# Block-causal attention and a feed-forward layer: splits, last blocks and a weight cast on other engines

## The chip, the cores and the metric

The kernel runs on one core of a Trainium2 chip, in one launch. Its engines work side by side, each through its own queue in order: TensorE (PE; its weight loads are listed as PEld), VectorE (DVE), ScalarE (ACT), GpSimd (POOL), and SyncE (SP), which here issues the DMAs. The metric is the device time of one execution in microseconds (us); less is better.

## The reference

Eight batches of eight heads, 576 tokens, 64 columns a head. The mask lets a block of 64 tokens see itself and all blocks before it. The attention's output, heads side by side (4608 x 512), goes through a layer of 2048 columns with a piecewise activation.

```python
scores = (1 / sqrt(64)) * q @ k.T              # per head, 576 x 576
scores = where(block_i >= block_j, scores, -1e9)   # blocks of 64
attn = exp(scores - max); attn /= (sum + 1e-9)
x = (attn @ v)  -> transposed to 4608 x 512
h = x @ w_in                                   # 512 x 2048
g = where(h >= 1, h, where(h <= -1, 0, (h + 1)**2 / 4))
out = g @ w_out                                # 2048 x 512
```

All inputs and the output are float32.

## The kernel before

Matrix products run on a shorter float type (fp32r). To keep precision, most operands are split into an upper part (hi, a cast) and a lower part (lo, the value minus its upper part), and a product is summed from hi and lo products. A split is thus always two operations, a cast and a subtraction, on the engines named in the code.

**Attention.** `Pair` is one batch and two heads; there are 32 pairs, worked through in eight steps each by `attention_steps`. For a pair, q and k are loaded as [128, 9, 64] (eight tiles for the two heads and a ninth for the two last blocks of 64 tokens), split by `split_q` and `split_k` on DVE (k's lower part on POOL, for the first pair on DVE), and transposed on PE by `turned` (two heads, q and k) and `turned_last` (the ninth tile). Each result lands in a PSUM bank and is copied by ACT into `qb` or `kb`; the half that holds one part is copied once more into `qa` or `ka`, by a DMA for `turned` and by DVE (L371) for `turned_last`. `qa` and `ka` also carry four rows with the mask. `product` sums two matmuls into the scores. `scores(j, g)` takes a head j and a group g of query tiles (g 0 holds 128 and 256 columns, g 1 holds 384, g 2 holds 512), `scores_last` the two heads' last blocks: a maximum by DVE (L414, L438, L442), the exponential by ACT (L418, L444), sum, EPS, reciprocal and scaling by DVE (L400, L401, L424, L448, L450). The probabilities `pr` are moved by a DMA into fp32r tiles (not for the first batch, which transposes `pr` itself), transposed by `turn` and `turn_last` (`ps_t`), and split for the product with v (`ps_av`, L500). Inside `turn_last` the last 64 columns go into a bank of their own and from there to `pc`. The first two batches (`plain`) keep the probabilities in one float32 part.

**Weights.** `convert` turns a 64-bit weight piece of 128x256 into hi and lo: a DMA, two ACT scalings (L165, L166), three DVE operations (L167, L170, L173), an addition on POOL (L179), the upper part's cast on ACT (L181), and the lower part's subtraction on POOL (L183). There are 64 pieces; they run beside the first pairs, 24 in the first 36 steps and the other 40 in the following 24 steps. Pieces have rings of three buffers. w_in stays in SBUF (`wih`, `wil`), w_out's parts go back to DRAM and are read again for each step.

**Feed-forward.** From step 36 on each attention step is followed by one step of the feed-forward: `ffn_in` (twelve matmuls into `ph`, activation by ACT and DVE, a split by ACT and POOL, L646 to L661) and, for the step before, `ffn_out` (twelve matmuls into `po`, L670 and L675). What is left runs after the attention.

**Order.** A scheduler places the instructions of each engine from their priorities in program order and from when buffers come free. Each engine then runs its list strictly in that order and waits where an operand isn't there. PSUM banks come from `work_bank`: while the feed-forward hasn't started, banks alternate between a ring of four (`po`) and a ring of three (`work`); later all come from the ring of three. `pr` has three buffers.

Of the kernel before, what the change touches and what calls it, by code (L numbers as in the profile page):

```python
# [8 lines left out]
F32 = mybir.dt.float32  # L9
# [14 lines left out]
def block_attn_then_ffn(  # L24
# [9 lines left out]
    nc = tc.nc  # L34
# [117 lines left out]
    def convert(n, source, hi, lo, done):  # L152
# [28 lines left out]
        nc.scalar.copy(hi(), w32)  # L181
# [69 lines left out]
    class Pair:  # L251
# [52 lines left out]

        def split_q(self):

            qn = self.nat.pop("q")[:, : 2 * NTL + 1, :]
            self.qs = att1.tile([P, 2 * NTL + 1, 2, D], F32R, tag="qs", name="qs")
            for c0, c1 in ((0, 2 * NTL), (2 * NTL, 2 * NTL + 1)):
                nc.vector.tensor_scalar_mul(self.qs[:, c0:c1, 0, :], qn[:, c0:c1, :], SCALE)  # L310
            nc.vector.scalar_tensor_tensor(
                out=self.qs[:, :, 1, :], in0=qn, scalar=SCALE,
                in1=self.qs[:, :, 0, :].bitcast(F32), op0=ALU.mult, op1=ALU.subtract,
            )

        def split_k(self):
            kn = self.nat.pop("k")[:, : 2 * NTL + 1, :]
            self.ks = att1.tile([P, 2 * NTL + 1, 2, D], F32R, tag="ks", name="ks")
            for c0, c1 in ((0, 2 * NTL), (2 * NTL, 2 * NTL + 1)):
                nc.vector.tensor_copy(self.ks[:, c0:c1, 1, :], kn[:, c0:c1, :])  # L320
            (nc.vector if self.first else nc.gpsimd).tensor_tensor(
                out=self.ks[:, :, 0, :], in0=kn, in1=self.ks[:, :, 1, :].bitcast(F32),
                op=ALU.subtract,
            )
# [16 lines left out]
        def turned(self, is_q, j):  # L341

            src, a, bt, hi0 = (self.qs, qa, qb, 0) if is_q else (self.ks, ka, kb, D)
            ps = work_bank("ps_qk")
            for t in range(NTL):
                nc.tensor.transpose(  # L346
                    ps[:, t * P : (t + 1) * P].bitcast(F32R), src[:, j * NTL + t, :, :], ident_r
                )

            turned = ps[:, :SM].rearrange("p (t c) -> p c t", t=NTL)  # L350
            nc.scalar.copy(bt[:, j, :SM].rearrange("p (c t) -> p c t", t=NTL), turned)  # L351
            if self.first and j == 0:
                nc.vector.tensor_copy(
                    a[:D, j, :SM].rearrange("p (c t) -> p c t", t=NTL), turned[hi0 : hi0 + D]
                )
            else:
                nc.sync.dma_start(
                    a[:D, j, :SM].bitcast(F32), bt[hi0 : hi0 + D, j, :SM].bitcast(F32)
                )

        def turned_last(self):
# [6 lines left out]
            for i, (a, bt, hi0) in enumerate(((qa, qb, 0), (ka, kb, D))):  # L368
                blocks = ps[:, i * P : (i + 1) * P].rearrange("p (h c) -> p h c", h=2)
                nc.scalar.copy(last_blocks(bt), blocks)  # L370
                nc.vector.tensor_copy(last_blocks(a)[:D], blocks[hi0 : hi0 + D])  # L371
# [55 lines left out]
        def scores_last(self):  # L427
# [14 lines left out]
            nc.vector.tensor_tensor(out=nm[:, 2:3], in0=nm[:, 0:1], in1=nm[:, 1:2], op=ALU.min)  # L442
# [5 lines left out]
            nc.vector.tensor_tensor(out=sm[:, 2:3], in0=sm[:, 0:1], in1=sm[:, 1:2], op=ALU.add)  # L448
            self.inverse(sm[:, 2:3])
# [15 lines left out]
        def turn(self, j, g):  # L465
# [4 lines left out]
            for c0 in range(0, n, P):  # L470
                self.transposed(ps[:, c0 : c0 + P], pr, c0, P)
            if g == 0:
# [8 lines left out]
        def turn_last(self):  # L481
            pr = self.pr.pop("last")
            ps = work_bank("ps_t")
            for c0 in range(0, SM, P):
# [4 lines left out]
            )  # L489
# [82 lines left out]
    def attention_steps():  # L572
# [11 lines left out]
        for i, cur in enumerate(pairs + [None]):  # L584
# [42 lines left out]
            cur.scores(1, 2)  # L627
            cur.attn_v(0)
            cur.turn(1, 0)
# [131 lines left out]
```

## Time and profile before

| | before |
|---|---|
| median of 3 runs | 1270.86 us (1270.6 to 1273.3) |
| the profiled execution | 1272.09 us |
| its span in the profile | 1270.3 us |
| granted PE clock, mean | 0.985 |
| busy in the span | PE 95%, PEld 80%, DVE 67%, ACT 55%, POOL 36% |

The profile is of one execution. A row of the groups gives the source line, the engine, the operation with output and input, the count, busy time in us, the mean ns of one, and behind the second bar how long the engine stood idle just before and what released it. A row of the waits gives the engine and line that waited, the one that released it, the total us, how often, and the longest. A row of the windows gives for a stretch of the span the busy us of PE, PEld, DVE, ACT and POOL with instruction counts, the granted PE clock, the share of the DMA engines and GB/s. A row of the timeline begins with the start and the duration in us. "idle" of an engine that nobody waits for costs nothing.

### The profile page before, as it was taken

The page shows a single profiled execution, that of the slowest core. Times are in us where ns is not written, and L with a number is a line of the kernel's source. Part 1 is how long each engine was busy: PE and PEld are TensorE (multiplying, and loading weights), DVE is VectorE, ACT ScalarE, POOL GpSimd, SP SyncE. Part 2 cuts the span into 40 slices and gives each one's busy share as a digit, 9 for nine tenths or more (in the row PEclk, how much of TensorE's full clock was granted, in tenths as well). Part 3 has the DMA queues.
Part 4 walks back from the last instruction along what each step waited for, and adds up shares of the span by engine and source line. Part 5 has one row for each costly group of instructions (what it writes and reads, how often), then busy time and mean ns, then how long its engine had stood idle before and what let it go on. Part 6 is the DMA issues. An engine that isn't in the chain of part 4 may idle for free.

```text
span 1270.3 us, 20591 instructions
## 1 busy us (share of the span) xinstructions
PE 1210.7 (95%) x6496; PEld 1018.4 (80%) x6496; DVE 856.4 (67%) x2164; ACT 701.3 (55%) x1827; POOL 456.3 (36%) x454
## 2 busy tenths in 40 slices
PE   5879887899999999999999999999999999999998
PEld 4667666688888888888888888888888888888886
DVE  8998877857776777777777777777777676222222
ACT  5877656546565655566556656555565564222222
POOL 3555655523332333333333333333333332222222
PEclk9888989899999999999999999999999999999999
DMA  5656666655444545564455545454445443322432
GB/s 157 182 165 213 196 228 210 212 184 173 148 152 147 191 144 161 158 193 149 148 162 168 178 141 161 153 181 143 152 154 184 151 132 117 127 92 97 133 100 100
DMA packets 146093, 201.30 MB, mean 158 GB/s; under 512 B 63152, under 2 KB 93872, under 8 KB 145984
## 3 DMA queue, kind: packets, MB, share of 16 engines
q1 hardware_dynamic: 145984, 199.98, 50.4%
q8 instruction: 52, 0.85, 0.3%
q14 instruction: 57, 0.47, 0.1%
HBM read 120.59 MB, written 17.83 MB: 109 GB/s over the span
## 4 chain that ended last, share of the span: by engine, by line
PE 68%; DVE 8%; ACT 4%; issue 3%; DMA 3%; POOL 2%; SPq 0%; ACTq 0%; POOLq 0%; DVEq 0%
PE ph L646 26%; PE po L670 16%; PE po L675 8%; PE ps_av L500 7%; PE ps_t L461 3%; PE ps_s L394 3%; PE ps_s L391 3%; ACT pr L418 2%; PE ps_qk L346 2%; DMA prr<-pr 2%; DVE t L656 2%; DVE nm L414 1%; DVE t L659 1%; DVE pr L424 1%; POOL work L179 1%
## 5 line engine op out<-in xcount | busy, mean ns | idle before, releaser
L661 POOL TENSOR_TENSOR gl<-t,gh 128x512 fp32r<-128x512 f32 x144 | 186.9, 1298 | 604.7 <-ACT gh L660 301.8
L670 PE MATMUL po<-wo,gh 128*128 128x512 f32 x1152 | 296.9, 399 | 0.1
L656 DVE SCALAR_TENSOR_TENSOR t<-t 128x512 f32<-128x512 f32 x144 | 112.9, 784 | 200.2 <-ACT t L655 198.5
L646 PE MATMUL ph<-xh,wih 128*128 128x512 f32 x576 | 237.6, 413 | 2.7 <-DVE t L659 1.8
L670 PEld LDWEIGHTS po<-wo,gh 128*128 128x128 f32 x1152 | 207.7, 188 | 39.3 <-ACT gh L660 0.6
L646 PE MATMUL ph<-xl,wih 128*128 128x512 f32 x576 | 227.4, 395 | 0.9 <-DVE xl L536 0.9
L646 PE MATMUL ph<-xh,wil 128*128 128x512 f32 x576 | 227.4, 395 | 0.0
L655 ACT ACTIVATE t<-ph 128x512 f32<-128x512 f32 x144 | 86.1, 598 | 184.7 <-PE ph L646 184.7
L418 ACT ACTIVATE pr<-ps_s,nm 128x128 f32<-128x128 f32 (+3 forms) x256 | 134.4, 529 | 50.6 <-DVE nm L414 50.3
L414 DVE TENSOR_REDUCE nm<-ps_s 128x1 f32<-128x128 f32 (+3 forms) x256 | 123.6, 485 | 48.7 <-PE ps_s L394 47.4
L675 PE MATMUL po<-wo,gl 128*128 128x512 f32 x576 | 155.3, 391 | 0.0
L660 ACT CAST gh<-t 128x512 fp32r<-128x512 f32 x144 | 89.6, 622 | 102.1 <-DVE t L659 101.7
L391 PE MATMUL ps_s<-ka,qa 68*128 68x288 f32 (+4 forms) x384 | 122.5, 334 | 9.1 <-ACT kb L351 4.2
L646 PEld LDWEIGHTS ph<-xh,wil 128*128 128x128 f32 x576 | 109.1, 189 | 24.1
L675 PEld LDWEIGHTS po<-wo,gl 128*128 128x128 f32 x576 | 108.1, 188 | 23.3
L646 PEld LDWEIGHTS ph<-xh,wih 128*128 128x128 f32 x576 | 109.1, 189 | 21.7 <-DVE t L659 2.4
L646 PEld LDWEIGHTS ph<-xl,wih 128*128 128x128 f32 x576 | 109.6, 190 | 20.2 <-DVE xl L536 1.5
L394 PE MATMUL ps_s<-kb,qb 128*128 128x288 f32 (+4 forms) x384 | 121.4, 323 | 0.0
L454 ACT CAST pb<-ps_t 128x512 fp32r<-128x512 f32 (+1 forms) x120 | 65.5, 546 | 85.6 <-PE ps_t L461 83.8
L424 DVE TENSOR_SCALAR pr<-pr,sm 128x128 f32<-128x128 f32 (+3 forms) x256 | 104.8, 430 | 4.0
L336 POOL TENSOR_TENSOR vsr<-vn,vsr 64x64 fp32r<-64x64 f32 (+1 forms) x96 | 72.8, 768 | 88.6 <-ACT vsr L335 88.6
L456 DVE TENSOR_TENSOR pb<-ps_t,pb 128x512 fp32r<-128x512 f32 (+1 forms) x120 | 75.6, 630 | 40.4 <-ACT pb L454 39.9
(101 smaller groups left out, 1961.4 us busy)
## 6 DMA issues: line engine op xcount, KB each, us to landing
wo<-wo_split SPq DMA_DIRECT2D x144, 512.0 KB, 3.4
prr<-pr SPq DMA_DIRECT2D x96, 192.0 KB, 2.7
prr<-pr SPq DMA_DIRECT2D x72, 256.0 KB, 2.6
out_dram<-ob SPq DMA_DIRECT2D x36, 256.0 KB, 3.9
qn<-in_q_dram SPq DMA_DIRECT2D x32, 256.0 KB, 2.9
kn<-in_k_dram SPq DMA_DIRECT2D x32, 256.0 KB, 2.9
bits<-in_moe_w_in_dram SPq DMA_DIRECT2D x32, 256.0 KB, 3.6
bits<-in_moe_w_out_dram SPq DMA_DIRECT2D x32, 256.0 KB, 3.2
```

Of the source, the lines that this page charges most:

```text
L391: nc.tensor.matmul(ps, qa[:KA, j, c0 : c0 + P], ka[:KA, j, k0 : k0 + n], start=first, stop=False)
L394: nc.tensor.matmul(ps, qb[:, j, c0 : c0 + P], kb[:, j, k0 : k0 + n], start=False, stop=last)
L414: nc.vector.tensor_reduce(out=nm[:, i : i + 1], in_=ps[:, cs], axis=AX.X, op=ALU.max, negate=True)
L418: nc.scalar.activation(pr[:, cs], ps[:, cs], AF.Exp, bias=nm[:, i : i + 1], scale=1.0, accum_out=sm[:, i : i + 1],)
L424: nc.vector.tensor_scalar_mul(pr[:, cs], pr[:, cs], sm[:, i : i + 1])
L500: nc.tensor.matmul(ps[:, lo_col:], vt, x, start=first and i == 0 and m == 0, stop=last and i == len(parts) - 1 and m == len(mov) - 1,)
L646: nc.tensor.matmul(ph, w[:, cc, fs], x[:, cc, xs], start=(cc == 0 and i == 0), stop=(cc == NCC - 1 and i == 2),)
L656: nc.vector.scalar_tensor_tensor(out=t_, in0=t_, scalar=1.0, in1=t_, op0=ALU.min, op1=ALU.mult)
L660: nc.scalar.copy(gh, t_)
L661: nc.gpsimd.tensor_tensor(out=gl, in0=t_, in1=gh.bitcast(F32), op=ALU.subtract)
L670: nc.tensor.matmul(po[tt], gh[:, ts_], wo[:, w, :], start=(fc == 0 and w == 0), stop=False)
L675: nc.tensor.matmul(po[tt], gl[:, ts_], wo[:, 0, :], start=False, stop=fc == NFC - 1)
```

## The change

- The split of q no longer scales: `split_qk` casts the raw value on DVE in one instruction of [128, 9, 64] (before: 8 tiles and the ninth apart), and the lower part of q is subtracted on POOL, as k's already was; the first pair keeps both on DVE. The factor 1/8 is applied by ACT when it evicts the transposed q.
- `turned_last`: the second copy of the last blocks is made by a DMA instead of by DVE (the first pair keeps DVE).
- `scores_last`: the minimum of two columns and the sum with EPS become forms with a column as a scalar; sum and EPS are one instruction.
- The transposes of the last 64 columns move from `turn_last` into `turn(1, 0)`, into free columns of its bank; `attn_v(0)` is called after `turn(1, 0)`.
- In `convert` the cast of the upper part goes from ACT to POOL.

```diff
@@ convert
-        nc.scalar.copy(hi(), w32)
+        nc.gpsimd.tensor_copy(hi(), w32)
@@ class Pair
+        def split_qk(self, name, side):
+            x = self.nat.pop(name)[:, : 2 * NTL + 1, :]
+            parts = att1.tile([P, 2 * NTL + 1, 2, D], F32R, tag=name + "s", name=name + "s")
+            hi, lo = parts[:, :, side, :], parts[:, :, 1 - side, :]
+            nc.vector.tensor_copy(hi, x)
+            (nc.vector if self.first else nc.gpsimd).tensor_tensor(
+                out=lo, in0=x, in1=hi.bitcast(F32), op=ALU.subtract
+            )
+            return parts
+
         def split_q(self):
-            qn = self.nat.pop("q")[:, : 2 * NTL + 1, :]
-            self.qs = att1.tile([P, 2 * NTL + 1, 2, D], F32R, tag="qs", name="qs")
-            for c0, c1 in ((0, 2 * NTL), (2 * NTL, 2 * NTL + 1)):
-                nc.vector.tensor_scalar_mul(self.qs[:, c0:c1, 0, :], qn[:, c0:c1, :], SCALE)
-            nc.vector.scalar_tensor_tensor(
-                out=self.qs[:, :, 1, :], in0=qn, scalar=SCALE,
-                in1=self.qs[:, :, 0, :].bitcast(F32), op0=ALU.mult, op1=ALU.subtract,
-            )
+            self.qs = self.split_qk("q", 0)
@@ turned
-            nc.scalar.copy(bt[:, j, :SM].rearrange("p (c t) -> p c t", t=NTL), turned)
+            scale = SCALE if is_q else 1.0
+            nc.scalar.mul(bt[:, j, :SM].rearrange("p (c t) -> p c t", t=NTL), turned, scale)
@@ turned_last
-                nc.scalar.copy(last_blocks(bt), blocks)
-                nc.vector.tensor_copy(last_blocks(a)[:D], blocks[hi0 : hi0 + D])
+                nc.scalar.mul(last_blocks(bt), blocks, 1.0 if i else SCALE)
+                if self.first:
...
+                else:
+                    nc.sync.dma_start(
+                        last_blocks(a)[:D].bitcast(F32), last_blocks(bt)[hi0 : hi0 + D].bitcast(F32)
+                    )
@@ scores_last
-            nc.vector.tensor_tensor(out=nm[:, 2:3], in0=nm[:, 0:1], in1=nm[:, 1:2], op=ALU.min)
+            nc.vector.tensor_scalar(
+                out=nm[:, 2:3], in0=nm[:, 0:1], scalar1=nm[:, 1:2], scalar2=None, op0=ALU.min
+            )
...
-            nc.vector.tensor_tensor(out=sm[:, 2:3], in0=sm[:, 0:1], in1=sm[:, 1:2], op=ALU.add)
-            self.inverse(sm[:, 2:3])
+            nc.vector.tensor_scalar(
+                out=sm[:, 2:3], in0=sm[:, 0:1], scalar1=sm[:, 1:2], scalar2=EPS,
+                op0=ALU.add, op1=ALU.add,
+            )
+            nc.vector.reciprocal(sm[:, 2:3], sm[:, 2:3])
@@ turn
+            if j == 1 and g == 0:
+                ps_c = ps[:BLK, n : n + P]
+                self.transposed(ps_c, self.pr.pop("last"), SM, BLK)
+                self.split(
+                    ps_c.rearrange("p (h c) -> p h c", h=2), *(x[:BLK] for x in self.pc)
+                )
@@ turn_last
-            ps = work_bank("ps_t")
-            self.transposed(ps[:BLK, :P], pr, SM, BLK)
-            self.split(
-                ps[:BLK, :P].rearrange("p (h c) -> p h c", h=2), *(x[:BLK] for x in self.pc)
-            )
@@ attention_steps
             cur.scores(1, 2)
+            cur.turn(1, 0)
             cur.attn_v(0)
-            cur.turn(1, 0)
```

The scheduler places everything anew, so the lists of the engines differ throughout. Three places follow. The new lines have other numbers: L310 and L311 are the cast and subtraction of `split_qk`, L342 is L346, L395 and L398 are L391 and L394, L422 is L418, L450 is L444, L463 is L454, L472 is L463, L348 is L351.

POOL, in the third pair, while weights are converted; of before:

```order
L321 TENSOR_TENSOR ks<-kn,ks 128x9x64
L179 TENSOR_TENSOR work<-work,bits 128x256 x2
L183 TENSOR_TENSOR ws<-work,ws 128x256
L179 TENSOR_TENSOR work<-work,bits 128x256 x2
L183 TENSOR_TENSOR ws<-work,ws 128x256
L183 TENSOR_TENSOR wil<-work,wih 128x256
```

and of the change:

```order
L179 TENSOR_TENSOR work<-work,bits 128x256
L181 CAST ws<-work 128x256
L311 TENSOR_TENSOR qs<-qn,qs 128x9x64
L183 TENSOR_TENSOR ws<-work,ws 128x256
L179 TENSOR_TENSOR work<-work,bits 128x256
L181 CAST ws<-work 128x256
L183 TENSOR_TENSOR ws<-work,ws 128x256
L311 TENSOR_TENSOR ks<-kn,ks 128x9x64
```

The cast L181 stands between addition and subtraction of its piece, and the subtraction of q has come into the list ahead of that of k.

ACT, in the second pair, from the eviction of its first transposed probabilities (`pa`) on; of before:

```order
L454 COPY pa_527<-ps_t 128x384
L418 ACTIVATE pr,sm<-ps_s,nm 128x512
L165 ACTIVATE work<-bits 128x256
L454 COPY pb_529<-ps_t 128x3x128
L181 CAST wih<-work 128x256
L166 ACTIVATE bits<-bits 128x256
L351 CAST qb<-ps_qk 128x512
L444 ACTIVATE pr,sm<-ps_s,nm 128x288 x2
L454 COPY pb_529<-ps_t 128x4x128
L181 CAST wih<-work 128x256
L418 ACTIVATE pr,sm<-ps_s,nm 128x128
```

and of the change:

```order
L463 COPY pa_521<-ps_t 128x384
L422 ACTIVATE pr,sm<-ps_s,nm 128x512
L463 COPY pb_523<-ps_t 128x3x128
L450 ACTIVATE pr,sm<-ps_s,nm 128x288 x2
L348 ACTIVATE qb<-ps_qk 128x512
L422 ACTIVATE pr,sm<-ps_s,nm 128x128
L422 ACTIVATE pr,sm<-ps_s,nm 128x256
L463 COPY pb_523<-ps_t 128x4x128
```

The two casts L181 are gone, the scalings L165 and L166 stand elsewhere, and the exponentials of `scores_last` (128x288) come ahead of q's eviction.

PE, in the second pair, from the scores of 384 columns of its second head on (`ps_t` of 64x128 are the transposes of the last 64 columns, `ps_qk` from `ks` those of the next pair's k); of before:

```order
L394 MATMUL ps_s<-kb,qb 128x384
L646 MATMUL ph<-xh,wil 128x512
L463 MATMUL ps_t<-ident_r,pr 128x128 x4
L463 MATMUL ps_t<-ident_r,pr 64x128
L346 MATMUL ps_qk<-ident_r,ks 128x128 x4
L391 MATMUL ps_s<-ka,qa 128x512
L394 MATMUL ps_s<-kb,qb 128x512
L463 MATMUL ps_t<-ident_r,pr 128x128 x3
```

and of the change:

```order
L398 MATMUL ps_s<-kb,qb 128x384
L342 MATMUL ps_qk<-ident_r,ks 128x128 x4
L472 MATMUL ps_t<-ident_r,pr 128x128 x4
L395 MATMUL ps_s<-ka,qa 128x512
L398 MATMUL ps_s<-kb,qb 128x512
L472 MATMUL ps_t<-ident_r,pr 128x128 x3
L472 MATMUL ps_t<-ident_r,pr 64x128
```

K's transposes now stand ahead of those of the last blocks' probabilities (`turn_last`), and the last 64 columns come behind the transposes of `turn(1, 0)`. The later pairs have the same order here, with matmuls of the feed-forward between: of before, k's transposes in the middle of an `ffn_in`; of the change, a whole `ffn_in` between k's transposes and the scores of 512 columns.

More of the change, by code (lines that the diff above doesn't have):

```diff
@@ L303, in load @@
             self.nat[name] = t_
-        def split_q(self):
-            qn = self.nat.pop("q")[:, : 2 * NTL + 1, :]
-            self.qs = att1.tile([P, 2 * NTL + 1, 2, D], F32R, tag="qs", name="qs")
-            for c0, c1 in ((0, 2 * NTL), (2 * NTL, 2 * NTL + 1)):
-                nc.vector.tensor_scalar_mul(self.qs[:, c0:c1, 0, :], qn[:, c0:c1, :], SCALE)
-            nc.vector.scalar_tensor_tensor(
-                out=self.qs[:, :, 1, :], in0=qn, scalar=SCALE,
-                in1=self.qs[:, :, 0, :].bitcast(F32), op0=ALU.mult, op1=ALU.subtract,
-            )
-        def split_k(self):
[L317 to L323, printed above, removed]
-            )
+        def split_qk(self, name, side):
[7 more added lines that the diff above has]
+            return parts
+        def split_q(self):
+            self.qs = self.split_qk("q", 0)
+        def split_k(self):
+            self.ks = self.split_qk("k", 1)
         def split_v(self):
@@ L471, in turn @@
                 self.transposed(ps[:, c0 : c0 + P], pr, c0, P)
+            if j == 1 and g == 0:
[3 more added lines that the diff above has]
+                    ps_c.rearrange("p (h c) -> p h c", h=2), *(x[:BLK] for x in self.pc)
+                )
             if g == 0:
@@ L481, in turn_last @@
         def turn_last(self):
-            pr = self.pr.pop("last")
+            pr = self.pr["last"]
             ps = work_bank("ps_t")
```

7 lines of the change are left out of this document (4 added, 3 removed).

## The prediction, made before the changed kernel was run

> **What bounds the kernel now.** I read the page first (its first line is quoted), then the busy time of each engine by stretch (the next lines, from the windows).
>
> ```profile
> span 1270.3 us, 20591 instructions
> core 0: us, PE busy (x) PEld busy (x) DVE busy (x) ACT busy (x) POOL busy (x), PEclk, DMA share, GB/s
> 0.00:128.00 128.00, 99.19 (x514) 80.35 (x515) 112.78 (x341) 93.76 (x280) 63.42 (x85) 0.91 0.60 178
> 128.00:256.00 128.00, 109.92 (x528) 85.81 (x528) 101.42 (x247) 79.12 (x224) 75.03 (x90) 0.95 0.68 216
> 256.00:640.00 384.00, 380.88 (x2164) 325.74 (x2162) 271.42 (x694) 224.53 (x579) 126.13 (x115) 1.00 0.52 162
> ```
>
> The reader is to see two stages. From 256 us on TensorE (PE) is busy 99% of the time: 384 - 380.88 leaves 3.1 us in that stretch. The change removes no matmul, so little can be won there. In the first 256 us, while the weights are converted beside attention, PE stands idle (128 - 99.19) + (128 - 109.92) = 28.8 + 18.1 = **46.9 us**, and its granted clock is 0.91 and 0.95. DVE is busy 112.78 + 101.42 = 214 us of them, 84%. A gain has to come from those 46.9 us. Next, what PE waited for there (25 rows; the first, some of the next, and the last):
>
> ```profile
> PE ps_qk L346 <- DVE ident_r L89: 7.6, 1, 7.6
> PE ps_t L463 <- DVE sm L400: 7.4, 3, 3.8
> PE ps_s L391 <- ACT kb L351: 4.2, 2, 3.9
> ...
> PE ps_qk L346 <- ACT pc L454: 0.2, 1, 0.2
> ```
>
> Summed over all 25 rows, 25.3 us end on DVE (7.6 of them are the start), 19.9 on ACT and 1.1 on a DMA. No one transfer or engine is late: both engines serve long queues in order, and PE gets its operand when its turn comes.
>
> **DVE's own work.** Groups of DVE instructions in the first 256 us:
>
> ```profile
> L167 DVE TENSOR_SCALAR work<-work 128x256 f32<-128x256 f32 x64 | 29.5, 465 | 12.6 <-ACT work L165 11.8 <-POOL wil L183 0.7
> L311 DVE SCALAR_TENSOR_TENSOR qs<-qn,qs 128x576 fp32r<-128x576 f32 x9 | 7.5, 830 | 0.0
> L310 DVE TENSOR_SCALAR qs<-qn 128x512 fp32r<-128x512 f32 x9 | 4.2, 468 | 0.2 <-DMA qn<-in_q_dram 0.2
> L320 DVE CAST ks<-kn 128x512 fp32r<-128x512 f32 x9 | 4.0, 439 | 0.0
> L320 DVE CAST ks<-kn 128x64 fp32r<-128x64 f32 x9 | 2.7, 301 | 2.1 <-DMA kn<-in_k_dram 2.1
> L310 DVE TENSOR_SCALAR qs<-qn 128x64 fp32r<-128x64 f32 x9 | 2.5, 277 | 0.0
> L371 DVE CAST ka<-ps_qk 64x128 fp32r<-64x128 f32 x8 | 2.3, 293 | 0.6 <-ACT kb L370 0.4
> L371 DVE CAST qa<-ps_qk 64x128 fp32r<-64x128 f32 x8 | 2.2, 272 | 0.0
> L442 DVE TENSOR_TENSOR nm<-nm 128x1 f32<-128x1 f32 x8 | 2.1, 268 | 0.0
> L448 DVE TENSOR_TENSOR sm<-sm 128x1 f32<-128x1 f32 x8 | 2.1, 261 | 3.0 <-ACT pr L444 3.0
> L400 DVE TENSOR_SCALAR sm<-sm 128x1 f32<-128x1 f32 x39 | 5.6, 144 | 2.4 <-ACT pr L418 2.1
> ```
>
> The q and k splits cost 7.5 + 4.2 + 4.0 + 2.7 + 2.5 = 20.9 us for nine pairs. Eight of these pairs keep two casts of 128x576 on DVE. Scaled from the 128x512 cast, one takes 0.44 x 576/512 = 0.49 us; the high end is one element a step, the 0.76 us that the first pair's 128x576 subtraction took. So 20.9 x 8/9 = 18.6 us becomes 16 x 0.49 = 7.8 (up to 12.2): -10.8 us (-6.4 at the dear end). I take the cheap end, the same operation.
>
> The Trainium skill, "VectorE: DVE Perf Modes", section "Mode 2×_2P", lets a one-source copy run two elements a cycle where the outermost dimension is even, or odd and equal on both sides; here it is 9 on both, so by that rule the cheap end holds, and the old cut into 8 + 1 bought nothing.
>
> The copies of the last blocks (L371) go to DMAs for seven of eight pairs: -(2.3 + 2.2) x 7/8 = -3.9. The minimum (L442) becomes a one-column scalar form at L400's 144 ns: -2.1 + 1.2 = -0.9. The sum and EPS (L448 and an L400) become one: -2.1. Together DVE loses **17.7 us** of own work (13.3 at the dear end). At the start two fewer operations precede ident_r: -0.4 us, which PE waits for outright (the 7.6).
>
> **What goes to POOL.** Its groups in the first 256 us, the one-input operation there is, and the two waits that the moved cast takes part in:
>
> ```profile
> L179 POOL TENSOR_TENSOR work<-work,bits 128x256 int32<-128x256 int32 x64 | 51.6, 811 | 66.8 <-ACT pr L418 12.0 <-DVE work L173 10.4 <-ACT qb L370 7.8
> L321 POOL TENSOR_TENSOR ks<-kn,ks 128x576 fp32r<-128x576 f32 x8 | 11.7, 1461 | 3.6 <-DVE ks L320 3.3
> L275 POOL MEMSET vs<- 128x320 f32 x16 | 5.6, 374 | 0.4 <-PE ps_av L500 0.4
> L124 POOL TENSOR_SCALAR_AFFINE_SELECT msel<-msel 4x256 f32<-4x256 f32 x1 | 0.4, 412 | 3.1 <-DVE qs L310 3.1
> L181 ACT CAST wih<-work 128x256 fp32r<-128x256 f32 x32 | 13.0, 411 | 18.8 <-POOL work L179 18.5
> L181 ACT CAST ws<-work 128x256 fp32r<-128x256 f32 x32 | 13.0, 410 | 12.7 <-POOL work L179 12.6
> POOL ws L183 <- ACT ws L181: 13.1, 18, 1.9
> POOL wil L183 <- ACT wih L181: 11.1, 20, 0.9
> ```
>
> No copy on POOL is in the trace. Between a memset (374 x 256/320 = 0.30 us) and two inputs (0.81 us), the one-input row of 256 columns took 0.41: I take that, 64 x 0.41 = 26 us (19 to 52). Eight q subtractions of 1.46 add 11.7. POOL rises from 63.42 + 75.03 = 138 to 176 us of 256 (169 to 202). But its wait for ACT's cast, 13.1 + 11.1 = 24 us, goes: a weight piece spends as long on POOL as before, a copy of 0.41 against 24/64 = 0.38 us of waiting.
>
> ACT loses 26.0 us of casts and the 18.5 + 12.6 = 31.1 us that it stood in its queue behind POOL's add: from 173 busy + 31 held to 147, a quarter less. The new order has exponentials and copies where casts stood. PE waits for ACT 19.9 us here; I take a third, **-6** (0 to -15). The eviction of q by a multiplication in place of a copy is the same pass; at most 0.03 us each (0.44 for L165 against 0.41 for L181), hidden on an engine with room.
>
> **What POOL's load gives back on DVE.** The same DVE form has very different lengths, and the long ones stand beside POOL:
>
> ```profile
> L170 DVE TENSOR_SCALAR work<-work x64: 268/294/1524, 11.1 to 246.4; 128x256 uint32<-128x256 uint32 x64
> 85.39 1.51 DVE L170 TENSOR_SCALAR work<-work 128x256 uint32<-128x256 uint32 x1
> 85.23 1.53 POOL L321 TENSOR_TENSOR ks<-kn,ks 128x576 fp32r<-128x576 f32 x1
> L424 DVE TENSOR_SCALAR pr<-pr,sm 128x512 f32<-128x512 f32 x15 | 11.2, 747 | 0.3
> L424 DVE TENSOR_SCALAR pr<-pr,sm 128x512 f32<-128x512 f32 x46 | 22.5, 488 | 0.8
> ```
>
> The 1.51 us L170 (minimum 0.268) ended with the 1.53 us POOL subtraction beside it. The last two rows are one form in the first 256 us and from 256 to 1024: 747 against 488 ns. L167 alone lost 64 x (0.465 - 0.268) = 12.6 us so, L170 by its range about as much; the widest L424 lost 15 x 0.259 = 3.9, the four widths about three times that; with some 7 for L173 and the rest I estimate 44 of DVE's 214 us to be such holding. If it grows with POOL's busy time (176/138 = 1.27), it gives back 12 us; 0 to 20 are the ends (short copies hold little; the long q subtraction holds most). DVE nets -17.7 + 12 = -6, with ends -18 and +7. PE's waits on DVE are on the path only in part: I take **-2** (+7 to -12).
>
> **Order, bank, buffers.** On PE, k's transposes now come before those of the last block's probabilities, which PE waited for: filler ahead of a wait, counted in the -6 and -2. Past 256 us the bank freed ends this wait:
>
> ```profile
> PE ps_qk L346 <- ACT pr L418: 2.9, 13, 0.3
> ```
>
> K's bank was the one that held the 384-column scores until their exponential; now it is the next in the ring, and the 512-column scores take the old one behind a whole ffn_in. **-2.5** (0 to -2.9). Against it, in the first four pairs (three pr buffers) the last blocks' probabilities live on until turn(1,0), so the exponential of scores(1,2) waits for four transposes: 0.4 us each, **+1.5** (0 to 4).
>
> The 62 new DMAs stand beside these rows (the like transfers of the page, and the timeline around one pair's last blocks):
>
> ```profile
> qa<-qb SPq DMA_DIRECT2D x63, 128.0 KB, 2.2
> 12.17 0.53 SPq L357 DMA_DIRECT2D qa<-qb  x1
> 79.27 0.23 PE L365 MATMUL ps_qk<-ident_r,ks 128*128 128x128 f32 x1
> 82.25 0.34 ACT L370 CAST kb<-ps_qk 128x128 fp32r<-128x128 f32 x1
> 85.12 0.39 PE L391 MATMUL ps_s<-ka,qa 68*128 68x288 f32 x1
> ```
>
> Transposes of the last blocks end at 79.5, scores_last reads the blocks at 85.12. ACT's order now has both casts in a row, about a microsecond sooner (81.5); two issues of 0.53 and 2.2 to landing end at 84.8. The cover is 0.3 us in the first pairs; behind the waiting DMA on SP stand weight and q loads, and PE's in-order queue behind scores_last. **+1** (0 if ACT is quicker; 1 us for seven pairs, +7, if SP's queue is late). Past 256 us PE has a whole ffn_in between, and I cost the DMAs at nothing there.
>
> **Sum.** The profiled execution took 1272.09 us, 1.2 above the median of the runs (1270.86). -0.4 - 6 - 2 - 2.5 + 1.5 + 1 = -8.4: 1263.7 against that execution, 1262.5 against the median; I say **1263**. The ends are -0.4 - 15 - 12 - 2.9 = -30 and 7 + 4 + 7 = +18.
>
> **Rivals.** *POOL becomes the engine that holds DVE.* Its place is the first 256 us; it decides from the point where the holding given back passes 17.7 us, that is at POOL busy 138 x (1 + 17.7/44) = 193 us, a copy of 0.68 us. With a copy at the two-input 0.81 us POOL is busy 202 us, the holding grows by 44 x 0.46 = 20, and a piece stays 0.43 us longer on POOL, so that ACT's relief buys nothing: +7 - 0.4 - 2.5 + 1.5 + 1 = +6.6, some **1279**. For it: the rows of 1.51 against 0.268 us, and a q subtraction twice as long on POOL as on DVE. Against it: the one-input row of 0.41, and the five removed DVE forms that were themselves held. Chance 0.21.
>
> The Trainium skill, "SBUF — State Buffer", section "Who interferes with whom", speaks against the change in this way: a copy, cast or scalar operation of DVE that uses both ports and any POOL instruction exclude each other for a whole instruction, whoever starts first. The trace agrees (1.51 us beside 1.53), so the rule carries this rival: by it new POOL work holds DVE as the old does, and the 12 us would be given back in full, not hidden.
>
> *The relief is hidden.* What paces the stage may be the weights' ring of three buffers, through DMA, ACT, DVE and POOL, whose length hardly changes (0.41 for 0.38 us). Then -6 and -2 go to nought: -0.4 - 2.5 + 1.5 + 1, about **1272**, no change. For it: the long list of small waits, none of them dominant. Chance 0.19.
>
> *More comes loose.* Shorter queues on ACT and DVE help each other, and PE's granted clock of 0.91 rises with fewer gaps: the good ends without the stray ones, -27, some **1245**. Chance 0.12.
>
> **How the numbers follow.** The forecast has 0.48. A measurement can tell about 0.2%, 2.5 us, from no change. Faster: forecast and third rival, 0.60; same: the hidden one, 0.19; slower: 0.21. The range of 1249 to 1277 leaves out half of the third rival and half of the first; the forecast's own is 1257 to 1269.
>
> **What would show it.** Right: POOL's L181 casts near 0.41 us, PE idle in the first 256 us near 39, ACT no longer waiting on POOL's L179, L167 and L170 means below 0.50, no wait of K's transposes on ACT past 256 us, qs casts at 0.5 us. Wrong: POOL casts above 0.68 us, or DVE's busy time in that stage above 214 us (first rival); PE's idle time unchanged with ACT well below 173 us busy (second); PE waiting at scores_last for a DMA (the +1); PE below 99% after 256 us, which no step here allows for.

## The result, and the profile after

The changed kernel took **1320.69 us** (median of 4 runs, 1313.06 to 1326.01) against 1271.41 for the kernel before beside it: a ratio of 1.038, 95% interval 1.033 to 1.044. The forecast was 1263 with a range to 1277. It is slower by 49 us. The profiled execution took 1322.58 us with a span of 1320.8.

Its first line and the busy time by stretch; the columns are those of the rows of before:

```profile
span 1320.8 us, 20732 instructions
0.00:128.00 128.00, 97.82 (x480) 79.19 (x481) 109.47 (x292) 79.58 (x236) 70.50 (x107) 0.85 0.56 162
128.00:256.00 128.00, 106.60 (x497) 83.10 (x497) 104.69 (x219) 65.86 (x180) 90.39 (x125) 0.91 0.63 201
256.00:640.00 384.00, 369.48 (x2069) 313.94 (x2069) 258.54 (x613) 215.20 (x564) 133.97 (x130) 0.99 0.54 162
```

PE's idle time in the first 256 us rose from 46.9 to 30.2 + 21.4 = 51.6 us, where 39 was forecast, and its granted clock there fell from 0.91 and 0.95 to 0.85 and 0.91. From 256 to 640 us it rose from 3.1 to 14.5: PE is no longer at 99%, which was named ahead as a thing that no step allowed for. What PE waits for in the first 256 us (18 rows; the first four and the last):

```profile
PE ps_qk L342 <- POOL qs L311: 11.0, 3, 5.5
PE ps_qk L342 <- DVE ident_r L89: 7.8, 1, 7.8
PE ps_qk L342 <- DVE xl L547: 6.5, 3, 3.1
PE ps_s L395 <- ACT kb L348: 3.6, 2, 1.9
...
PE ps_s L395 <- ACT pb L463: 0.2, 1, 0.2
```

Summed over the 18 rows, ACT fell from 19.9 to 9.5 us, as hoped, and DVE from 25.3 to 23.6; new are 12.5 us on POOL (11.0 of them on the subtraction of q, first row), and 5.8 end on DMAs, up from 1.1. One late operand took the place of another. Past 266 us, the first row of the waits of before and then of the change:

```profile
PE ps_t L461 <- DMA prr<-pr: 3.2, 5, 1.6
```

```profile
PE ps_t L470 <- DMA prr<-pr: 21.2, 24, 2.4
```

The transposes of probabilities (`turn`) wait for the DMA that copies `pr` into fp32r tiles. The reader should ask who delays that copy. The timeline shows it, around one pair of the change; SPq is SP's queue of DMA issues:

```profile
642.27 0.49 SPq L246 DMA_DIRECT2D prr<-pr  x1
642.85 0.62 SPq L373 DMA_DIRECT2D ka<-kb  x1
643.56 1.10 SPq L285 DMA_DIRECT2D vn<-in_v_dram  x2
644.71 0.65 SPq L289 DMA_DIRECT2D vn<-in_v_dram  x1
645.46 0.54 SPq L295 DMA_DIRECT2D qn<-in_q_dram  x1
646.04 2.11 SPq L300 DMA_DIRECT2D qn<-in_q_dram  x2
648.25 0.53 SPq L295 DMA_DIRECT2D kn<-in_k_dram  x1
648.83 0.48 SPq L300 DMA_DIRECT2D kn<-in_k_dram  x1
649.40 0.54 SPq L246 DMA_DIRECT2D prr<-pr  x1
...
652.43 0.51 PE L470 MATMUL ps_t<-ident_r,prr 128*128 128x128 f32 x4 [1.63 <-DMA prr<-pr]
653.12 3.12 PE L681 MATMUL po<-wo,gh 128*128 128x512 f32 x8
```

The same place of the kernel before:

```profile
714.89 0.48 SPq L246 DMA_DIRECT2D prr<-pr  x1
715.41 0.58 SPq L285 DMA_DIRECT2D vn<-in_v_dram  x1
...
719.23 0.48 SPq L300 DMA_DIRECT2D kn<-in_k_dram  x1
719.80 0.54 SPq L246 DMA_DIRECT2D prr<-pr  x1
...
723.04 0.47 PE L461 MATMUL ps_t<-ident_r,prr 128*128 128x128 f32 x4
723.68 2.08 PE L670 MATMUL po<-wo,gh 128*128 128x512 f32 x8
```

In these rows SP issues one DMA after the other, most in about 0.5 to 0.65 us each. Between the second copy of 384 columns, `scores(0, 1)`, and that of 512, `scores(0, 2)`, stand the loads of the next pair. From one copy to the other it was 719.80 - 714.89 = 4.9 us, and is 649.40 - 642.27 = 7.1 (medians of the 24 pairs: 4.9 and 6.5): a new last-block DMA and one more v load stand in between, and two short q loads take 2.11 us in place of 1.15. PE then stands idle for 1.63 us, and the eight matmuls behind it take 3.12 us, against 2.08 at this place of before. The window over them shows what goes with that, a granted clock (third column from the end) of 0.64:

```profile
652.90:656.30 3.40, 3.40 (x14) 2.77 (x13) 1.51 (x4) 2.41 (x7) 1.28 (x1) 0.64 0.49 152
```

This gave the theory for the experiments, **theory Q**: past 256 us the time is lost because SP issues the copy of `scores(0, 2)` late, and PE pays for the wait and for the clock behind it. The rivals: **P**, POOL's new work (the cast, q's subtraction) holds PE or DVE; **R**, the bank less and the moved columns make PE wait; and, for the new DMAs, that they load the DMA engines.

### The profile page after: what moved, and what is told of

It is laid out like the page before. It is cut to its first block, busy times and chain, and to the rows that moved or that the text cites. A ratio compares the mean times of both kernels' runs of the same rounds, so it can differ in the third digit from the quotient of the medians.

```text
span 1320.8 us, 20732 instructions
## 1 busy us (share of the span) xinstructions
PE 1229.5 (93%) x6496; PEld 1030.2 (78%) x6496; DVE 850.1 (64%) x1975; ACT 678.7 (51%) x1763; POOL 504.6 (38%) x549
## 4 chain that ended last, share of the span: by engine, by line
PE 71%; DVE 10%; DMA 10%; ACT 3%; issue 2%; SPq 2%; POOL 1%; ACTq 0%; DVEq 0%; POOLq 0%
PE ph L657 23%; PE po L681 18%; PE po L686 8%; PE ps_av L511 8%; DMA prr<-pr 6%; PE ps_t L470 4%; PE ps_s L395 3%; PE ps_s L398 3%; PE ps_qk L342 2%; DVE pr L428 2%; DVE nm L418 1%; DVE t L667 1%; DVE work L170 1%; DVE work L173 1%; PE ps_t L472 1%
## 5 line engine op out<-in xcount | busy, mean ns | idle before, releaser
L672 POOL TENSOR_TENSOR gl<-t,gh 128x512 fp32r<-128x512 f32 x144 | 190.5, 1323 | 621.7 <-ACT gh L671 406.4
L681 PE MATMUL po<-wo,gh 128*128 128x512 f32 x1152 | 304.8, 406 | 0.1
L681 PEld LDWEIGHTS po<-wo,gh 128*128 128x128 f32 x1152 | 212.2, 192 | 41.0 <-ACT gh L671 0.6
L667 DVE SCALAR_TENSOR_TENSOR t<-t 128x512 f32<-128x512 f32 x144 | 104.8, 728 | 204.1 <-ACT t L666 202.8
L418 DVE TENSOR_REDUCE nm<-ps_s 128x1 f32<-128x128 f32 (+3 forms) x256 | 123.5, 485 | 56.8 <-PE ps_s L398 55.9
L422 ACT ACTIVATE pr<-ps_s,nm 128x128 f32<-128x128 f32 (+3 forms) x256 | 134.6, 530 | 42.7 <-DVE nm L418 41.3
L463 ACT CAST pb<-ps_t 128x512 fp32r<-128x512 f32 (+1 forms) x120 | 65.2, 543 | 137.9 <-PE ps_t L470 137.8
L395 PE MATMUL ps_s<-ka,qa 68*128 68x288 f32 (+4 forms) x384 | 124.3, 338 | 6.2 <-ACT kb L348 3.6
L428 DVE TENSOR_SCALAR pr<-pr,sm 128x128 f32<-128x128 f32 (+3 forms) x256 | 120.9, 493 | 6.1 <-DVE sm L405 0.5
L398 PE MATMUL ps_s<-kb,qb 128*128 128x288 f32 (+4 forms) x384 | 122.8, 327 | 0.0
L470 PEld LDWEIGHTS ps_t<-ident_r,prr 128*128 128x128 f32 x600 | 64.9, 139 | 50.5 <-issue 14.5
```

What stands on the lines that cost most here:

```text
L395: nc.tensor.matmul(ps, qa[:KA, j, c0 : c0 + P], ka[:KA, j, k0 : k0 + n], start=first, stop=False)
L398: nc.tensor.matmul(ps, qb[:, j, c0 : c0 + P], kb[:, j, k0 : k0 + n], start=False, stop=last)
L418: nc.vector.tensor_reduce(out=nm[:, i : i + 1], in_=ps[:, cs], axis=AX.X, op=ALU.max, negate=True)
L422: nc.scalar.activation(pr[:, cs], ps[:, cs], AF.Exp, bias=nm[:, i : i + 1], scale=1.0, accum_out=sm[:, i : i + 1],)
L428: nc.vector.tensor_scalar_mul(pr[:, cs], pr[:, cs], sm[:, i : i + 1])
L470: nc.tensor.transpose(out.bitcast(F32R), src, ident_r)
```

## The experiments

All are timed against the kernel before on the same chip, where its medians lie between 1270.9 and 1272.1 us; the changed kernel's 1320.7 is the other measure.

**Parts taken out or alone.** Four kernels. e1 is the change without its new DMAs; e2 the kernel before with these alone; e3 and e4 give q's lower part back to DVE, the weight's cast back to ACT.

e1:

```diff
-                if self.first:
-                    nc.vector.tensor_scalar_mul(
-                        last_blocks(a)[:D], blocks[hi0 : hi0 + D], 1.0 if i else SCALE
-                    )
-                else:
-                    nc.sync.dma_start(
-                        last_blocks(a)[:D].bitcast(F32), last_blocks(bt)[hi0 : hi0 + D].bitcast(F32)
-                    )
+                nc.vector.tensor_scalar_mul(
+                    last_blocks(a)[:D], blocks[hi0 : hi0 + D], 1.0 if i else SCALE
+                )
```

e2 makes the opposite edit, without the scale, in the kernel before. e3 and e4:

```diff
-            (nc.vector if self.first else nc.gpsimd).tensor_tensor(
+            (nc.vector if self.first or name == "q" else nc.gpsimd).tensor_tensor(
```

```diff
-        nc.gpsimd.tensor_copy(hi(), w32)
+        nc.scalar.copy(hi(), w32)
```

> The changed kernel with one part undone: the last blocks are copied by DVE again, no DMA of 64x2x64. Theory Q (SP's queue): past the conversion stage the changed kernel's PE waited 21.2 us in 24 waits for prr DMAs, which are issued late because the two new DMAs stand on SP ahead of the q, k and v loads and of that prr; each such idle also lowers PE's clock for a few us. Without them PE's waits on prr fall back towards the 3.2 us of before and the time falls by about 35 us, to 1278 to 1290. Rival B (bank and order): the moved transposes and the new PE order make the wait; then the time stays at 1313 to 1325. Rival P (POOL): same, 1313 to 1325.

> The kernel before with one part of the change alone: the last blocks' second copy by DMA. Theory Q: 1295 to 1310, with PE waiting on prr DMAs past the conversion stage. Rivals B and P: 1268 to 1274, since neither the bank nor POOL is touched.

> The changed kernel with the subtraction of q's lower part on DVE for every pair. Theory P (POOL's queue): in the conversion stage PE waited 11.0 us in 3 waits for q's subtraction, behind weight pieces on POOL; without it the stage loses 10 to 15 us, total 1303 to 1312. Theory that q's subtraction only holds DVE by the shared port: DVE busy in the first 266 us unchanged and 1315 to 1325.

> The changed kernel with the cast of the weight's upper part on ACT again. If the cast on POOL is what delays the weight pieces and q's subtraction: 1303 to 1312. If POOL's queue is late because of the q subtraction's place behind pieces that wait for other engines, the cast hardly matters: 1315 to 1325, or longer, since ACT waits for POOL again.

Measured: e1 **1366.9** us (ratio 1.075), e2 **1312.1** (1.034), e3 **1313.0** (1.033), e4 **1319.4** (1.037).

In e2 the DMAs alone, with the order that comes with them, cost 41 us, 2 more than theory Q allowed, with 17.9 us of waits on `prr`. But its timeline shows a second reason for a late copy, and one that isn't SP's queue (L429 is L424 of before):

```profile
458.85 1.42 POOL L321 TENSOR_TENSOR ks<-kn,ks 128x576 fp32r<-128x576 f32 x1
458.88 1.61 DVE L429 TENSOR_SCALAR pr<-pr,sm 128x384 f32<-128x384 f32 x1
```

The last cast of k now stands ahead of this scaling in DVE's list, where it stood behind it before, so k's subtraction on POOL starts together with the scaling. Of the 48 scalings of 384 columns past 266 us, 22 last about 1.6 us like this one, each beside k's subtraction; the mean of the form is 978 ns, against 424 before, where none took 0.9 us. The copy of `scores(0, 1)` waits for the held scaling, and SP's list stands behind that copy. By the medians of the pairs the copy of `scores(0, 2)` is issued 1.9 us later after its scores than before: 1.3 us of it is already there at the copy of `scores(0, 1)`, and 0.6 comes between the two copies, with one more load on SP. So e2 shows that the DMAs are not free, but speaks only in part for Q's reason.

e3 came out between its two ranges, 8 us below the change; 24 of its scalings are held in the same way (1.2 us). e4 is in the range that said that the cast hardly matters; its runs lie between 1310.8 and 1324.4 us, so no effect of the cast can be told from them. e1 missed by 77 us, on the far side. Its timeline says why:

```profile
655.98 0.48 SPq L246 DMA_DIRECT2D prr<-pr  x1
...
660.35 1.93 SPq L300 DMA_DIRECT2D kn<-in_k_dram  x2
662.37 0.53 SPq L669 DMA_DIRECT2D wo<-wo_split  x1
663.00 1.82 SPq L246 DMA_DIRECT2D prr<-pr  x3
...
667.47 0.72 PE L465 MATMUL ps_t<-ident_r,prr 128*128 128x128 f32 x4 [3.48 <-DMA prr<-pr]
668.50 3.10 PE L676 MATMUL po<-wo,gh 128*128 128x512 f32 x8
```

With the DMAs gone the scheduler ordered SP anew, and now both last kn loads and `wo` stand ahead of the copy. So e1 changed two things and can't be read as the price of the DMAs. It made a sharper question: which part moves the copy? In SP's lists of the change's parts, alone and combined, each kernel that has the split of q and k without the new DMAs has the copy behind both short kn loads and `wo` (in 21 of the 24 pairs), and none of the others has. The split touches no DMA at all.

**The split alone, and the change without split and DMAs.** g1 keeps the cast on POOL, the small forms and the bank; g2 is the kernel before with `split_qk` and its scale alone.

> The changed kernel without the split of q's lower part on POOL (with its scale on ACT) and without the last blocks' copies by DMA; the cast on POOL, the small scalar forms, the transposes of the last 64 columns in turn(1, 0) and the bank less remain. On SP's queue the pr copies of scores(0, 2) then stand where they stood before, with only the last kn loads and wo among them. Theory Q (the 50 us are lost because SP issues the pr copies of scores(0, 2) behind the loads of the next pair): 1258 to 1275 us, PE's waits in turn on prr under 8 us in all past 266 us, and the last subtraction of a weight piece (L183) starts before 254 us. Rival theory R (the bank less and the columns moved into turn(1, 0) make PE wait): 1300 us or more. Rival P (POOL's casts of weights hold DVE): 1280 or more, most of it in the first 256 us.

> The kernel before with one part alone: q's and k's split by one function, q's subtraction on POOL, the scale in the moves of the turned parts. Nothing in it touches a DMA, but on SP's queue it puts the pr copies of scores(0, 2) behind the last two kn loads and wo. Theory Q: 1335 to 1370 us, as slow as the changed kernel without its last-block DMAs (1366.9), with PE's waits on prr over 40 us in all past 266 us. Rival R (the bank and the columns): 1262 to 1280. Rival P (q's subtraction on POOL is the cost, by its own duration in the first stage): 1275 to 1285, waits on prr under 10 us.

Measured: g1 **1273.9** us (1.0019, interval 1.0003 to 1.0035), g2 **1359.8** (1.069). Both as theory Q had it. R falls: all of the bank's part is in g1. So does the cast as a part of P, since g1 has it, too.

**The loads on another queue.** g3 is the change, g4 the kernel before, with `load`'s DMAs of v, q and k (from the third batch on) on ACT's queue.

```diff
+            queue = nc.sync if self.plain else nc.scalar
...
-                    nc.sync.dma_start(
+                    queue.dma_start(
```

> The changed kernel whole, with the loads of v, q and k of the pairs after the first batch's issued from ACT's queue in place of SP's: no load stands ahead of the pr copies on SP. Theory Q: the prr waits past 266 us fall from 21 us to under 8 and the time to 1270 to 1292 us; what is left above 1271 is the first stage, whose last weight piece comes 15 us later than before. If ACT's own queue pays for nine issues of a pair, the waits on ACT pr rise and it ends near 1300. Rivals R and P, to which the loads' queue is nothing: 1310 to 1325.

> The control of the run beside it: the kernel before with the same loads on ACT's queue. Theory Q: the 3.2 us of waits on prr go at most, ACT pays for the issues: 1262 to 1277 us. If this is as much faster against before as the other is against the changed kernel, the loads' place is a gain of its own and says nothing on the change.

Measured: g3 **1317.2**, g4 **1288.8** us. Both missed Q's ranges, and g3's time lies where the rivals had put it. But the control lost 17 us by the same move, so the two can't decide: the waits on `prr` were 15.1 us in g3, and 18.1 in the control, where before had 3.2. The copy was now issued 0.03 us after its operand was there, and still came late. What a transfer takes in flight is part of its lateness, and the loads now flew beside it: where the profile tells its landing, this copy took 3.9 us in g3 and 4.4 in g4 (medians), against 2.9 before. In g3 the operand itself came 1.2 us later than before, too.

**The copy on another queue.** i1 is the change with one DMA of each pair moved, the copy of `scores(0, 2)`; i2 the kernel before and i5 the split alone (g2) with the same.

```diff
-            self.pr[j, g] = as_float32r(pr[:, : cols[-1].stop], self.plain) if self.hop else [pr]
+            queue = nc.scalar if (j, g) == (0, 2) else nc.sync
+            self.pr[j, g] = as_float32r(pr[:, : cols[-1].stop], self.plain, queue) if self.hop else [pr]
```

> The changed kernel whole, with one DMA of each pair moved: the pr copy of scores(0, 2) (128x512) is issued from ACT's queue, not from SP's, so that neither loads nor wo stand ahead of it; the rest of SP's order is that of the changed kernel. Theory Q (the place of that copy on SP's queue costs PE its waits, and each wait the clock behind it): PE's waits on prr past 266 us fall from 21 us to under 6 and the time from 1320 to 1272 to 1295 us; what is left above 1271 is the first stage, untouched here. Theory B (the last-block DMAs and the others load the DMA engines, or PE waits for DVE and POOL): 1310 to 1325. ACT, which now waits for DVE's scaling of pr before its next move, may cost 0 to 8 us.

> The control: the kernel before with the same copy of scores(0, 2) on ACT's queue. There it stood early enough on SP (3.2 us of PE's waits on prr in all): 1265 to 1278 us. If it gains 20 us or more here too, the copy's queue is a gain of its own.

> The kernel before with the split of q and k alone (which put the pr copy of scores(0, 2) behind kn and wo on SP's queue: 1359.8 us), and that copy issued from ACT's queue. Theory Q: nearly all 88 us come back, 1266 to 1290 us, and PE's waits on prr fall from 48 us to under 8. Theory P (q's subtraction on POOL itself is what the split costs): 1330 or more.

Measured: i1 **1299.3** (4 above its range), i2 **1292.5** (a miss: 15 above), i5 **1281.0** us: of the split's 88 us, 79 come back by the place of one DMA in a pair. The end of DVE's scaling stayed where it was (3.7 us after the scores in g2 and i5), so it is the copy's way that was worth them. i1 keeps every DMA of the change, so the number of DMAs alone is not what its 21 us (1320.7 to 1299.3) were. The first row of PE's waits past 266 us on `prr`, in g2 and then in i5:

```profile
PE ps_t L460 <- DMA prr<-pr: 48.2, 20, 3.6
```

```profile
PE ps_t L461 <- DMA prr<-pr: 1.9, 4, 1.0
```

The following table puts the runs together. For the 24 pairs past 266 us it is read from the timelines, as medians: from the end of DVE's scaling of the 512 columns to the issue of their copy; from that end to when PE has nothing else before their transposes; and the mean wait of PE there that ended with the copy. The last columns split the span into PE's busy time (6496 matmuls in each) and the rest.

| run | issue after | PE ready after | wait | PE busy | PE idle |
|---|---|---|---|---|---|
| before | 0.36 us | 3.62 us | 0.10 us | 1210.7 us | 59.6 us |
| g1 | 0.35 | 3.65 | 0.03 | 1209.5 | 59.9 |
| the change | 2.02 | 4.16 | 0.66 | 1229.5 | 91.3 |
| e1 | 2.08 | 3.92 | 2.09 | 1250.5 | 114.3 |
| e2 | 0.86 | 2.76 | 0.70 | 1221.9 | 85.1 |
| g2 | 2.06 | 3.94 | 1.97 | 1250.7 | 108.9 |
| g4 | 0.03 | 3.77 | 0.75 | 1214.8 | 71.5 |
| i2 | 0.03 | 3.78 | 0.47 | 1211.8 | 77.0 |
| i5 | 0.03 | 3.77 | 0.03 | 1219.3 | 60.6 |
| i1 | 0.03 | 4.00 | 0.00 | 1225.1 | 73.6 |

Where the copy was issued 2 us late PE waited, and PE's busy time rose by up to 40 us for the same matmuls, since their clock was lower: of g2's 89 us of span, 49 are idle time and 40 are clock. In g2's trace the granted clock is 0.5 in 21 stretches past 266 us, 72 us in all, which makes 36 of these 40; before and i5 have no such stretch there. In the change there are five of them, which cost 8.5 us.

The delay of the issue is not all: the change and g2 issue the copy equally late (2.02 and 2.06), but PE waits three times as long in g2. Where PE waited, its transposes began 3.0 us after the issue in the change, and 4.1 us in g2 (medians of 22 pairs each). Right ahead of the copy stand one short kn load in the change, and in g2 two of them and the 512 KB of `wo`; that these make the longer way was not tried by itself. e2 is a case of its own: there the operand is late, so that PE is ready only 2.76 us behind it.

The two controls show the flight, too. From ACT's queue the copy leaves at once, but flies among the loads: the rows of its DMA (KB each, median us to landing) in i2, then in i5:

```profile
prr<-pr ACTq DMA_DIRECT2D x24, 256.0 KB, 4.3
```

```profile
prr<-pr ACTq DMA_DIRECT2D x24, 256.0 KB, 3.7
```

0.03 + 4.3 is past the 3.78 at which PE is ready, 0.03 + 3.7 is not. In the kernel before, the 72 copies of this size land in 2.6 us on SP's queue; the copy of `scores(0, 2)` itself took 2.9 us there (median of the nine whose landing the profile tells). The Trainium skill, "DMA: Bandwidth & Descriptors", section "Issuing engines are not separate DMA queues", says that DMAs issued by ScalarE, SyncE or GpSimd all run on the same 16 DMA engines; these rows fit that. Why the flight differs between i2 and i5 was not tried.

**The first stage.** There the last subtraction of a weight piece came 15.8 us later in the change (264.4 against 248.6; 258.2 in e2). i6 is i1 with the new DMAs left out in the first two batches; j1 is i5, and j2 is i6, with q's subtraction on DVE in these batches.

i6, in `turned_last`:

```diff
-                if self.first:
+                if self.plain:
```

j1 and j2, in `split_qk`:

```diff
-            (nc.vector if self.first else nc.gpsimd).tensor_tensor(
+            (nc.vector if self.first or (self.plain and name == "q") else nc.gpsimd).tensor_tensor(
```

> As the first run here, and the last-block DMAs left out for the pairs of the first stage (DVE copies there, as before). If those DMAs hold the first stage's other DMAs on SP's queue (the weights' pieces and the pr copies), the last weight piece's subtraction starts 5 to 9 us earlier than in the first run, and the time is 5 to 12 us less; if q's subtraction on POOL is what holds the pieces, no more than 3 us less.

> The split of q and k alone with the pr copy of scores(0, 2) on ACT's queue (1281.0 us), and in the pairs of the first stage (the first two batches) q's subtraction on DVE in place of POOL. What is left over 1271 there lies in the first stage, whose last weight piece came 8.7 us later than before. If q's subtraction on POOL (24 ahead of pieces and in PE's way) is what holds that stage: 1268 to 1275 us, the last piece before 253 us. If it is the scale in the moves of the turned parts, or the new order alone: 1278 to 1284, the last piece after 255 us.

> The changed kernel with three places mended: the pr copy of scores(0, 2) on ACT's queue, last blocks by DMA only from the third batch on, and q's subtraction on DVE in the first two batches. Without the third it took 1288.4 us. If all of the loss is these three: 1272 to 1282 us. If POOL's subtraction of q in the first stage costs nothing: 1285 to 1291.

Measured: i6 **1288.4**, 10.9 below i1, with the last piece 5 us sooner (259.8 against 264.8). j2 **1283.4**, 5.0 below i6, between its two ranges and 1.4 above the one in which these three places were all of the loss. j1 **1280.1**: the last piece came where the theory had it, in i5 first and then in j1,

```profile
257.31 1.42 POOL L183 TENSOR_TENSOR ws<-work,ws 128x256 fp32r<-128x256 f32 x2
```

```profile
249.04 0.73 POOL L183 TENSOR_TENSOR ws<-work,ws 128x256 fp32r<-128x256 f32 x1
```

but the median of the time fell by only 0.9 us, within the runs' scatter. So q's subtraction on POOL, with its order, does hold the pieces back by 8 us; that these 8 us are lost at the end isn't shown. The split alone, with its copy and its subtraction mended, still has 8 us that no run explains. The profile of i5 tells where they are: PE's idle time is nearly that of before (60.6 and 59.6), its busy time is 8.6 us longer, and its granted clock in the first 128 us is 0.83 against 0.91. Why the clock is lower there stays open.

Of the change's 49 us, then, 21 came back with the place of the copy (i1), 11 more without the new DMAs in the first two batches (i6), and 5 more with q's subtraction (j2). The other 12 stay open.

**The bank's term.** j3 is the kernel before with the moved columns and the small forms alone.

> The kernel before with two parts of the change: the last 64 columns' transposes in turn(1, 0), so a bank less, and the small scalar forms; SP's order stays that of before. By the prediction's terms (-2.5 us for K's transposes, which no longer wait for ACT, and about -0.5 for the small forms): 1266 to 1271 us, with the 2.9 us of waits on ACT's pr gone. If the bank gives nothing: 1271 to 1274.

Measured: **1272.1** against 1272.06 us, ratio 1.0006 (0.9995 to 1.0018). The wait on ACT is gone, as in the change, and this row took its place (3.2 us before):

```profile
PE ps_t L466 <- DMA prr<-pr: 5.4, 13, 0.9
```

No kernel tried beats the one before.

## Why the prediction was wrong

- **The step that failed**: "Past 256 us PE has a whole ffn_in between, and I cost the DMAs at nothing there." It looked at who reads the new DMAs' data. It did not look at what is queued behind them on SP, where the copy of `scores(0, 2)` stands: in the change that copy is issued 1.7 us later behind its operand, PE waits 21.2 us for the copies of `pr` in place of 3.2, and 21 of the 49 us come back when this copy has another queue (i1). The DMAs alone, with their order, cost 41 us (e2), though there the larger part of the delay is a scaling that POOL holds. In the first stage I had priced them at +1, and +7 if SP's queue is late, for PE waiting at `scores_last`. They cost 10.9 us there (i6 against i1), and in none of PE's 18 rows does `scores_last` wait for a DMA: the term was too small and had the wrong reader.
- **What no step held**: that the split reorders SP. It adds no DMA, so its effect on SP was taken as none; alone it costs 88 us, and 79 of them return when one copy has a way of its own (i5). The two parts together cost less (49) than the split alone: the copy leaves as late, but the DMAs bring another order, in which only one short kn load, not two and `wo`, stands right ahead, and it arrives about 1 us sooner. The prediction read lists of PE, ACT and POOL, not that of SP.
- **ACT's relief, -6**: the operation was right and the gain was not. ACT went from 172.9 to 145.4 us busy (147 forecast), no longer waits for POOL's L179, and PE's waits on it halved. But 12.5 us on POOL and 4.7 more on DMAs took their place, and with the cast back on ACT no other time can be told (e4; g1 with the cast on POOL took 1273.9 us, j3 without it 1272.1).
- **DVE, -2**: busy time in the first 256 us is 214.2 us, the same as before, where -6 was expected (and 61 of the 64 pieces were done, so per piece it rose). What POOL's load gives back was sized well: with the cast back on ACT (e4) DVE is busy 200.8 us in this stretch with as many instructions (511 and 510), so the casts on POOL held it by 13 us, where 12 were taken. What was too large is the own work saved: at the dear end, 13.3 us, it is eaten up by these 13. The cast of 128x576 was forecast at 0.49 us, the cheap end; the rows of the change give the dear one:

```profile
L310 DVE CAST qs<-qn 128x576 fp32r<-128x576 f32 x8 | 5.9, 740 | 0.0
L181 POOL CAST wih<-work 128x256 fp32r<-128x256 f32 x32 | 14.4, 450 | 1.7
L181 POOL CAST ws<-work 128x256 fp32r<-128x256 f32 x29 | 13.7, 472 | 5.2 <-DMA wo_split<-ws 2.4 <-PE po L686 1.3
L311 POOL TENSOR_TENSOR qs<-qn,qs 128x576 fp32r<-128x576 f32 x7 | 10.8, 1540 | 1.3 <-DVE qs L310 0.9 <-DVE sm L404 0.5
L167 DVE TENSOR_SCALAR work<-work 128x256 f32<-128x256 f32 x61 | 25.8, 423 | 16.7 <-ACT work L165 16.6
```

  The old cut into 512 and 64 columns took 0.41 + 0.29 us (k's, past 256 us), so the one instruction bought nothing. What the prediction took from the Trainium skill, "VectorE: DVE Perf Modes", section "Mode 2×_2P", two elements a cycle with nine rows on both sides, does not hold for this cast: its 740 ns are the length of the two-source form of this size, 0.76 us, which the prediction had named as the dear end.
- **POOL's copy, 0.41 us**: 0.450 and 0.472, well below the 0.68 at which the first rival decides. That rival's side, slower, came true, its mechanism did not: POOL's casts held DVE (the 13 us above), but g1, with the same casts, is at the level of before. Of the two means that were to lie below 0.50, L167's fell from 0.465 to 0.423, and L170's rose from 0.447 to 0.508. The Trainium skill, "SBUF — State Buffer", section "Who interferes with whom", has a DVE scalar operation that uses both ports and POOL exclude each other for a whole instruction. That did not decide the change's time; e2's scalings of 1.6 us beside POOL fit it.
- **The bank, -2.5**: the wait went (2.9 us, none left) and the time did not (j3). PE's waits on the copies rose by 2.2 us in its place.
- **The start, -0.4**: PE's wait for ident_r is 7.8 us, 7.6 before; nothing came of it. **The pr buffers, +1.5**, were not tried by themselves.

## What to carry to other kernels

Where all DMAs go through one queue, read that queue's list before and after as one reads PE's: a part that touches no DMA can move a copy on which the bound engine waits. For each copy near the path, write down three numbers, the delay from operand to issue, the flight, and when the consumer is ready; here 0.36 + 2.9 against 3.62 us left 0.4 us, and in the change 2.02 + 3.0 against 4.16 is 0.9 us too much. Then look whether the operand itself has moved, as in e2. A wait taken from a full engine can be worth nothing if the next operand was only hidden behind it.

## What was unexpected of the hardware

Idle time of PE shorter than 2 us could go with a lower clock of what followed: 1.63 us of waiting, then 3.4 us at a granted 0.64, eight matmuls in 3.12 us for 2.08. Not every such wait in the change did so: behind 2.44 us, the longest, the eight took 2.09. In g2 all of PE's 20 waits of 2 us and more past 266 us were followed by a stretch at 0.5. In i2 the copy on ACT's queue was issued 0.3 us sooner than on SP's, but took 4.3 us to land in place of about 2.9. And a DVE scaling that takes 0.41 us took 1.61 beside a POOL subtraction that started 0.03 us ahead of it (e2).
